# An attention and expert kernel: a new order of loads, slots and units in its first third

## The chip, the cores and the metric

The kernel runs on one core of a Trainium2 chip. The metric is device time in microseconds (us) of one execution. TensorE multiplies matrices, VectorE (DVE in the rows), ScalarE (ACT) and GpSimd (POOL) work element by element, and SyncE (SP) issues the loads. Each of them executes its instructions in a fixed order, and an instruction that waits holds back all behind it on that engine. For SP this means that a load that waits for its buffer holds back all later loads.

## The reference

Three blocks follow each other. The input is q, k, v of shape (4 batches, 8 heads, 576 positions, 64).

```
q_d, k_d, v_d = means over groups of 4 positions        # 144 positions
out_up    = repeat(softmax(q_d k_d^T / 8) v_d, 4)
out_local = softmax(q k^T / 8 where |i - j| < 4) v
x = (out_up + out_local)  as 2304 tokens x 512
x = (sigmoid(x w_gate) * (x w_val)) w_out                # 512 -> 1536 -> 512
logits = x phi                                           # 32 slots, 8 experts x 4
d = softmax of logits over the tokens;  slot_in = d^T x
slot_out[e] = relu(slot_in[e] w1[e]) w2[e]
result = softmax of logits over the slots  times slot_out
```

The weights w_gate, w_val and w_out arrive as 64-bit floats; the kernel converts them itself.

## The kernel before

*Attention.* Two heads make a pair; there are 4 pairs (NP) in a batch, numbered k = 0 to 15. The downsampled attention of a pair is `g_items(k)`: load, pool the groups of four (`g_pool`: q and k by reductions on VectorE or additions on POOL, v on POOL), scores (psD), three exponentials on ScalarE, transposes (psE), product with v (psV), copy to od. The local attention of a tile t of 128 tokens is `l_items(t)` or `attend(t)`: load lq, lk, lv (`load_tile`), scores (psS), mask and softmax in the tile t, transposes (psT), product with lv (psO), sum with od into x, and the split of x into a high part xh (ScalarE) and a low part xl (POOL).

*Units.* The first expert layer is cut into 6 chunks u of 256 columns (w_gate and w_val together 512 columns). `unit(t, u)` is 12 matmuls of 512 columns into psM: high times high, high times low and low times high over four blocks of 128 rows; then a tanh on ScalarE and one step on VectorE give h. Before that, `load_w(u)` loads the chunk's raw 64-bit values and `prep_w` converts them, in four pieces of a chunk: one step on ScalarE and three on VectorE (`to_f32`, result wf), a cast to whi on ScalarE, and the rest wlo on POOL.

*wo.* The last weights are loaded in 12 blocks of 128 rows (`load_wo`, `prep_wp`), converted in the same way, written to a buffer in main memory (wod), transposed (psW), multiplied with phi, and closed after every fourth block.

*Slots.* The pool wp has 12 slots of 2048 floats per partition. Each of whi and wlo of a chunk takes one for good. The pairs of batches 0 and 1 take two each, for a time, so later chunks wait for slots that pairs give back. The raw weights have 4 buffers of 512 KB, wf has 3, lq and lk together 4, lv one, the tile t two.

*Order.* The program text runs: loads of pairs 0 to 3 and tile 0, the four pairs, tile 0; then for each chunk u the loads of the next chunk and the next tile, the preparation, one or two of the pairs 4 to 7, the next tile, and the units that have become possible. Chunks 4 and 5 are prepared but their units come later, between the blocks of wo, which are scheduled with a higher priority. After that tiles 4 to 14 go through all six chunks in a hand-made order of half-units, with the work of other tiles beside them, then the tail with w1 and w2. A scheduler may move instructions ahead on each engine where nothing forbids it, but the loads marked by `keep_in_program_order` keep their order on SP, and so do TensorE's instructions from tile 4's units on.

Of the kernel before, what the change touches and what calls it, by code (L numbers as in the profile page):

```python
# [15 lines left out]
P = 128  # L16
# [6 lines left out]
def kernel(  # L23
# [91 lines left out]
    HPAIRS = ()  # L115
    odb = {}
    QP = 2 * NP

    def load_pair(k):
        b, p = divmod(k, NP)  # L120
        d = G[k] = {}
        if b < 2:
            pl, tag = (hp, "h") if k in HPAIRS else (wp, "w")
            m = pl.tile([P, 1536], F32, name="g0", tag=tag)
            o = 2 * S
            d["q"], d["k"] = m[:, :S], m[:, S:o]
            d["td"] = m[:, :3 * SD].rearrange("p (b w) -> p b w", w=SD)
            d["qd"], d["kd"] = m[:, o:o + 160], m[:, o + 160:o + 160 + SD]
            m = pl.tile([P, 1536], F32, name="g1", tag=tag)[:KH]
            v = m[:, :8 * P].rearrange("g (c r e) -> g c r e", c=2, r=4)  # L130
            d["v"] = [v[:, c] for c in range(2)]
            d["pt"] = m[:, :6 * P].rearrange("g (c b q) -> g c b q", c=2, b=3)
            d["vd"] = m[:, 8 * P:10 * P].rearrange("g (c e) -> g c e", c=2)
        else:
            gl = st["gl"]
            d["q"] = gl.tile([P, S], F32, name="gq", tag="gq")
            d["k"] = gl.tile([P, S], F32, name="gk", tag="gk")
            v = gl.tile([KH, 2, 4, P], F32, name="gv", tag="gv")
            d["v"] = [v[:, c] for c in range(2)]
            d["pt"] = gl.tile([KH, 2, 3, P], F32, name="gpt", tag="gpt")  # L140
            d["qd"] = gl.tile([P, 160], F32, name="qd", tag="qd")
            d["kd"] = gl.tile([P, SD], F32, name="kd", tag="kd")
            d["vd"] = gl.tile([KH, 2, P], F32, name="vd", tag="vd")
            d["td"] = gl.tile([P, 3, SD], F32, name="td", tag="td")
# [19 lines left out]
    def g_pool(k):  # L164
# [4 lines left out]
        for c in range(2):  # L169
            v = d["v"][c]  # L170
            nc.gpsimd.tensor_tensor(out=v[:, 0:2], in0=v[:, 0:2], in1=v[:, 2:4], op=ALU.add)
            nc.gpsimd.tensor_tensor(out=d["vd"][:, c], in0=v[:, 0], in1=v[:, 1], op=ALU.add)
# [40 lines left out]
    def g_av(k):  # L213
# [3 lines left out]
        for c in range(2):  # L217
            for h in range(2):
                r = slice(64 * h, 64 * h + 64)
                tmm(  # L220
                    ps[r, :SD], lhsT=d["vd"][:, c, r], rhs=d["pt"][:, c, :, 64 * h:64 * h + 48],
# [865 lines left out]
```

## Time and profile before

| | |
|---|---|
| median of 3 runs | 642.84 us (642.78 to 646.41) |
| the profiled execution | 645.25 us |
| its span, first to last instruction | 643.4 us |
| TensorE busy | 565.2 us (88%) |
| VectorE, ScalarE, POOL busy | 259.3, 261.9, 122.7 us |
| DMA | 93.50 MB, mean 145 GB/s |
| chain of waits, by engine | PE 65%, DVE 11%, DMA 8%, ACT 8%, SPq 3%, issue 3% |

The page gives busy times over the whole span and the chain that ended last. The kernel has stages with different limits, so the windows (busy time of each engine in a stretch) and the timeline (instructions in order of time) are read beside the page. A count such as x102 is the number of instructions in a group; a releaser is what an instruction waited for last.

### The profile page before, as it was taken

The numbers are of one execution on the slowest core, as the hardware profiler recorded it, in microseconds if no ns is written. First come the engines' busy times: TensorE is split into PE (matmuls) and PEld (weight loads), VectorE is DVE, ScalarE is ACT, GpSimd is POOL, SyncE is SP. The second block draws the span as 40 slices with busy tenths as digits, with TensorE's granted clock in tenths as the row PEclk, the third lists the DMA queues.
The fourth block names the chain that finished last, engine by engine and source line by source line (L and its number), as shares of the span: only waits on it lengthen the run. The fifth ranks groups of instructions, "written<-read, shape, count | busy, mean of one in ns | idle before, by whom it ended". The sixth has DMA issues, their size and how long they took to land.

```text
span 643.4 us, 11691 instructions
## 1 busy us (share of the span) xinstructions
PE 565.2 (88%) x4595; PEld 420.5 (65%) x4595; DVE 259.3 (40%) x596; ACT 261.9 (41%) x856; POOL 122.7 (19%) x169
## 2 busy tenths in 40 slices
PE   2557686888958999999999999999999999998974
PEld 2445564666835677777777777877877777763343
DVE  3697739464357233334243243233233211133032
ACT  2376253644345335355354443444243321133132
POOL 3343526431000332113032121000000100000000
PEclk9957787899975699999999999999999999999997
DMA  8846744260379423113032121182000276659999
GB/s 224 227 135 201 219 122 139 73 200 0 86 256 331 150 69 90 52 56 108 1 107 64 48 70 36 20 262 53 19 1 19 93 284 236 238 213 357 366 299 286
DMA packets 86230, 93.50 MB, mean 145 GB/s; under 512 B 8392, under 2 KB 65864, under 8 KB 86176
## 3 DMA queue, kind: packets, MB, share of 16 engines
q1 hardware_dynamic: 79904, 88.43, 44.4%
q10 hardware_dynamic: 6272, 4.33, 2.1%
q8 instruction: 36, 0.59, 0.4%
q14 instruction: 18, 0.15, 0.1%
HBM read 84.88 MB, written 7.86 MB: 144 GB/s over the span
## 4 chain that ended last, share of the span: by engine, by line
PE 65%; DVE 11%; DMA 8%; ACT 8%; SPq 3%; issue 3%; POOL 0%; ACTq 0%; DVEq 0%; POOLq 0%
PE psM L99 39%; PE psL L99 5%; PE psO L99 4%; ACT t L313 4%; PE psH L104 4%; SPq L109 3%; PE psT L104 2%; DVE wf L398 2%; PE psEH L99 2%; DMA g<-in_kT_dram 2%; DVE wf L401 2%; DVE wf L397 2%; PE psS L99 2%; DMA raw<-in_wg_dram 2%; PE psW L99 1%
## 5 line engine op out<-in xcount | busy, mean ns | idle before, releaser
L99 PE MATMUL psM<-whi,xh 128*128 128x512 f32 x432 | 185.5, 429 | 16.3 <-DVE h L484 8.3
L99 PE MATMUL psM<-whi,xl 128*128 128x512 f32 x432 | 173.6, 403 | 4.7 <-POOL xl L374 4.7
L99 PE MATMUL psM<-wlo,xh 128*128 128x512 f32 x432 | 174.2, 403 | 0.0
L99 PEld LDWEIGHTS psM<-whi,xh 128*128 128x128 f32 x432 | 83.4, 193 | 44.7 <-DVE h L484 11.4
L484 DVE SCALAR_TENSOR_TENSOR h<-th,psM 128x256 f32<-128x256 f32 x108 | 44.8, 416 | 157.5 <-ACT th L483 155.3
L99 PEld LDWEIGHTS psM<-whi,xl 128*128 128x128 f32 x432 | 83.1, 192 | 26.6 <-POOL xl L374 6.3
L483 ACT ACTIVATE th<-psM 128x256 f32<-128x256 f32 x108 | 40.9, 382 | 139.7 <-PE psM L99 139.2
L99 PEld LDWEIGHTS psM<-wlo,xh 128*128 128x128 f32 x432 | 83.6, 194 | 15.0 <-issue 0.6
L313 ACT ACTIVATE t<-t,mxl 128x70 f32<-128x70 f32 x144 | 48.9, 341 | 26.7 <-DVE mxl L302 26.4
L374 POOL TENSOR_TENSOR xl<-x,xh 128x512 fp32r<-128x512 f32 x18 | 23.8, 1324 | 160.6 <-ACT xh L373 160.6
L501 ACT COPY hT<-psH 128x512 f32<-128x512 f32 x54 | 31.7, 586 | 31.2 <-PE psH L104 30.8
L432 POOL TENSOR_TENSOR wlo<-wf,whi 128x512 fp32r<-128x512 f32 x24 | 33.6, 1407 | 36.3 <-ACT whi L431 35.3
L104 PE MATMUL psH<-ident,h 128*128 128x128 f32 x216 | 34.5, 281 | 1.0 <-ACT hT L501 0.8
L396 ACT ACTIVATE wf<-raw 128x512 f32<-128x512 f32 x36 | 24.1, 672 | 22.0 <-DMA raw<-in_wg_dram 12.6
L401 DVE SCALAR_TENSOR_TENSOR wf<-raw,wf 128x512 uint32<-128x512 uint32 x36 | 31.9, 889 | 0.8
L104 PEld LDWEIGHTS psH<-ident,h 128*128 128x128 f32 x216 | 25.9, 144 | 8.3 <-ACT hT L501 1.5
L398 DVE SCALAR_TENSOR_TENSOR wf<-raw,wf 128x512 uint32<-128x512 uint32 x36 | 28.5, 792 | 0.8
L397 DVE TENSOR_SCALAR wf<-wf 128x512 uint32<-128x512 uint32 x36 | 20.6, 574 | 18.1 <-ACT wf L396 17.9
L313 ACT ACTIVATION_READ_ACCUMULATOR t<-t,mxl 128x1 f32 x144 | 27.0, 187 | 0.0
L99 PEld LDWEIGHTS psS<-lk,lq 64*64 64x64 f32 x576 | 22.2, 143 | 5.9 <-issue 5.4
L99 PE MATMUL psS<-lk,lq 64*64 64x70 f32 x576 | 25.4, 236 | 0.0
L335 ACT COPY pt<-psT 70x512 f32<-70x512 f32 x36 | 19.4, 583 | 11.9 <-PE psT L104 11.6
(137 smaller groups left out, 718.3 us busy)
## 6 DMA issues: line engine op xcount, KB each, us to landing
ew<-in_w_dram SPq DMA_DIRECT2D x15, 1024.0 KB
raw<-in_wg_dram SPq DMA_DIRECT2D x12, 512.0 KB
raw<-in_wv_dram SPq DMA_DIRECT2D x12, 512.0 KB
raw<-in_wo_dram SPq DMA_DIRECT2D x12, 512.0 KB
ewp<-in_w_dram SPq DMA_DIRECT2D x22, 256.0 KB
lv<-in_vp_dram SPq DMA_DIRECT2D x16, 280.0 KB
lk<-in_kT_dram SPq DMA_DIRECT2D x16, 268.0 KB
lq<-in_qT_dram SPq DMA_DIRECT2D x16, 256.0 KB
```

The source lines that it names most:

```text
L99: ins = nc.tensor.matmul(*args, **kw)
L104: ins = nc.tensor.transpose(*args)
L313: nc.scalar.activation(out=tt[:, i], in_=tt[:, i], func=AF.Exp, bias=d["mx"][:, i:i + 1], accum_out=d["sl"][:, i:i + 1])
L374: nc.gpsimd.tensor_tensor(out=xl[t], in0=x, in1=xh[t].bitcast(F32), op=ALU.subtract)
L396: nc.scalar.activation(out=dst, in_=hi.bitcast(F32), func=AF.Copy, scale=2.0 ** -112)
L397: nc.vector.tensor_scalar(out=u, in0=u, scalar1=3, scalar2=None, op0=ALU.logical_shift_left)
L398: nc.vector.scalar_tensor_tensor(out=u, in0=lo, scalar=29, in1=u, op0=ALU.logical_shift_right, op1=ALU.bitwise_or)
L401: nc.vector.scalar_tensor_tensor(out=u, in0=hi, scalar=0x80000000, in1=u, op0=ALU.bitwise_and, op1=ALU.bitwise_or)
L432: nc.gpsimd.tensor_tensor(out=wlo[u][:, :, sl], in0=f, in1=whi[u][:, :, sl].bitcast(F32), op=ALU.subtract)
L483: nc.scalar.activation(out=th, in_=ps[:, :FU], func=AF.Tanh, scale=0.5)
L484: nc.vector.scalar_tensor_tensor(out=hs[t][:, u * FU:(u + 1) * FU], in0=th, scalar=1.0, in1=ps[:, FU:], op0=ALU.add, op1=ALU.mult)
L501: nc.scalar.copy(out=d[i], in_=ps.rearrange("p (j q) -> p j q", q=P))
```

## The change

The first third is written anew; the main part and the tail keep their text.

- Pairs 0 to 7 take one slot each (`load_qk`), and the values of all four pairs of a batch are loaded at once into two slots (`load_v`) and pooled by four wide additions on POOL (`v_pool`).
- A raw weight load takes 256 columns at once: rows of 2 KB, two buffers of 1 MB. `load_wo` takes two blocks at once.
- lv has two buffers, the tile t one.
- The loop over chunks is written out: after each preparation the next chunk's load and a tile's load are issued, pairs 4 to 7 are loaded together ahead of chunk 3 and worked together behind tile 3, units run by chunk, the units of chunk 4 run before wo, those of chunk 5 beside it. The blocks of wo have no priority of their own and their first loads stand ahead of tile 5's.

```
+    def load_qk(k):
+        b, p = divmod(k, NP)
+        d = G[k] = {}
+        m = wp.tile([P, 2048], F32, name="g0", tag="w")
...
+        load(d["q"], qT[b, p])
+        load(d["k"], kT[b, p, :, 3:3 + S])
+    def load_v(b):
+        for c in range(2):
+            v = GV[b, c] = wp.tile([P, 4 * DM], F32, name="g1", tag="w")[:KH].rearrange("g (r e) -> g r e", r=4)
+            load(v, vp[b, 3 + c * 4 * KH:3 + (c + 1) * 4 * KH, :].rearrange("(g r) e -> g r e", r=4))
+    def v_pool(b):
+        for c in range(2):
+            v = GV[b, c]
+            nc.gpsimd.tensor_tensor(out=v[:, 0:2], in0=v[:, 0:2], in1=v[:, 2:4], op=ALU.add)
+            nc.gpsimd.tensor_tensor(out=v[:, 2], in0=v[:, 0], in1=v[:, 1], op=ALU.add)
...
-        d["v"] = ld.tile([KW, 2, DM], F32, name="lv", tag="lv", bufs=1)
+        d["v"] = ld.tile([KW, 2, DM], F32, name="lv", tag="lv", bufs=2)
...
-            d["t"] = sf.tile([P, 2, NP, KW], F32, name="t", tag="t", bufs=2)
+            d["t"] = sf.tile([P, 2, NP, KW], F32, name="t", tag="t")
...
-            for h in range(2):
-                raw = raws[u, g, h] = stg.tile([P, NC, HU, 2], U32, name="raw", tag="raw", bufs=4)
+            raw = raws[u, g] = stg.tile([P, NC, FU, 2], U32, name="raw", tag="raw", bufs=2)
...
-        raw = raws[f] = stg.tile([P, DM, 2], U32, name="raw", tag="raw", bufs=4)
+        raw = raws[f] = stg.tile([P, 2, DM, 2], U32, name="raw", tag="raw", bufs=2)
...
+    attend(0); prep_chunk(0); load_w(1); load_tile(2); unit(0, 0)
+    attend(1); prep_chunk(1); load_w(2); load_tile(3)
+    for t, u in ((0, 1), (1, 0), (1, 1)):
+        unit(t, u)
+    for k in range(NP, 2 * NP):
+        load_qk(k)
+        if k == NP + 1:
+            load_v(1)
+    attend(2); prep_chunk(2); load_w(3)
+    for t, u in ((0, 2), (1, 2), (2, 0), (2, 1), (2, 2)):
+        unit(t, u)
+    v_pool(1)
+    attend(3)
+    for k in range(NP, 2 * NP):
+        for it in g_items(k):
+            it()
+        unit(K0 - 1, k - NP) if k < NP + 3 else None
+    prep_chunk(3); load_w(4)
...
+    for t in range(K0):
+        unit(t, 3)
+    prep_chunk(4); load_w(5)
+    for t in range(K0):
+        unit(t, 4)
+    prep_chunk(5)
+    load_wo(0); load_wo(2)
     for t in range(K0, TS):
         for it in list(l_items(t))[:-1]:
             it()
...
     for t in range(K0):
-        for u in range(UL, NU):
-            unit(t, u)
...
+        unit(t, NU - 1)
+        for f in range(3 * t, 3 * t + 3):
+            prep_wp(f)
+            if f % 2 and f + 3 < NF:
+                load_wo(f + 3)
```

(Calls that stand on lines of their own are joined by semicolons in the last part.)

The order of instructions, at three places. First SP's queue where the last chunk and wo are loaded; raw are the weights, lq, lk, lv a tile's inputs. Before:

```order
L109 DMA raw<-in_wg_dram 128x4x256 x2
L109 DMA raw<-in_wv_dram 128x4x256 x2
L109 DMA lq<-in_qT_dram 128x4x128
L109 DMA lk<-in_kT_dram 128x4x134
L109 DMA lv<-in_vp_dram 70x2x512
L109 DMA lq<-in_qT_dram 128x4x128
L109 DMA lk<-in_kT_dram 128x4x134
L109 DMA lq<-in_qT_dram 128x4x128
L109 DMA lk<-in_kT_dram 128x4x134
L109 DMA lv<-in_vp_dram 70x2x512
L109 DMA raw<-in_wo_dram 128x1024 x4
```

and now:

```order
L109 DMA raw<-in_wg_dram 128x4x512
L109 DMA raw<-in_wv_dram 128x4x512
L109 DMA sel_95<-in_cst_dram 128x128
L109 DMA phis<-in_phi_dram 128x4x32
L109 DMA raw<-in_wg_dram 128x4x512
L109 DMA raw<-in_wv_dram 128x4x512
L109 DMA raw<-in_wo_dram 128x2x1024 x2
L109 DMA lq<-in_qT_dram 128x4x128
L109 DMA lk<-in_kT_dram 128x4x134
L109 DMA lv<-in_vp_dram 70x2x512
```

The two loads of chunk 5 had three tiles with their lq, lk and lv, or parts of them, between them and wo; now wo follows chunk 5 at once, and nothing of a tile stands between chunks 4 and 5 either.

Second VectorE where pairs 4 to 7 are pooled (g_... are the pairs; L158 is now L173, the last step of a conversion L401 is now L416). Before, around pair 4:

```order
L401 SCALAR_TENSOR_TENSOR wf<-raw,wf 128x512 x2
L359 TENSOR_TENSOR x<-psO,od 128x512
L158 TENSOR_REDUCE g_487<-g_487 128x144
L397 TENSOR_SCALAR wf<-wf 128x512
L398 SCALAR_TENSOR_TENSOR wf<-raw,wf 128x512
L401 SCALAR_TENSOR_TENSOR wf<-raw,wf 128x512
```

and now, around pairs 6 and 7:

```order
L412 TENSOR_SCALAR wf<-wf 128x512
L498 SCALAR_TENSOR_TENSOR h<-th,psM 128x256
L413 SCALAR_TENSOR_TENSOR wf<-raw,wf 128x512
L173 TENSOR_REDUCE g_589<-g_589 128x144
L416 SCALAR_TENSOR_TENSOR wf<-raw,wf 128x512
L304 SCALAR_TENSOR_TENSOR t<-psS,mask 128x280
L374 TENSOR_TENSOR x<-psO,od 128x512
L173 TENSOR_REDUCE g_592<-g_592 128x144
L304 SCALAR_TENSOR_TENSOR t<-psS,mask 128x280
```

The conversion's last step stood ahead of the only pooling there; now the pooling of pair 6 stands between the last two steps of a conversion, and that of pair 7 between the two mask steps (L304) of a tile.

Third TensorE in the stage of wo: psW are the blocks of wo, whi and wlo a chunk's weights in the units. Before:

```order
L99 MATMUL psM<-wlo_397,xh 128x512
L99 MATMUL psM<-whi_396,xl 128x512
L104 MATMUL psW<-ident,wf 128x128 x4
L99 MATMUL psW_1475<-hT,phis 32x128 x4
L104 MATMUL psW<-ident,wf 128x128 x8
L99 MATMUL psW_1475<-hT,phis 32x128 x4
L104 MATMUL psW<-ident,wf 128x128 x4
L99 MATMUL psW_1475<-hT,phis 32x128 x4
```

and now, from the sixth of the twelve blocks:

```order
L99 MATMUL psO<-pt,lv 64x64 x16
L99 MATMUL psW_1471<-sel_95,part 128x32 x4
L99 MATMUL psW_1571<-hT,phis 32x128 x4
L104 MATMUL psW<-ident,wf 128x128 x3
L99 MATMUL psM<-whi_1261,xh 128x512
L99 MATMUL psM<-wlo_1262,xh 128x512
L99 MATMUL psM<-whi_1261,xl 128x512
L104 MATMUL psW<-ident,wf 128x128 x4
L99 MATMUL psW_1571<-hT,phis 32x128 x4
```

Before, the blocks stood together without a unit between them; now six units stand between the first six blocks, here the last three matmuls of them, and the later blocks follow alone.

## Rows read from the trace of the kernel before

**Rows 1.** Windows: stretch, busy us (instructions) per engine, clock, DMA share, GB/s.

```profile
0.00:221.00 221.00, 161.75 (x1151) 121.17 (x1152) 130.69 (x234) 101.80 (x307) 71.26 (x88) 0.81 0.57 169
221.00:643.40 422.40, 403.46 (x3447) 299.34 (x3446) 128.57 (x362) 160.12 (x549) 51.40 (x82) 0.99 0.42 133
147.00:181.00 34.00, 32.46 (x255) 25.87 (x254) 11.60 (x27) 12.38 (x48) 3.45 (x3) 1.00 0.17 41
181.00:214.00 33.00, 22.65 (x154) 14.81 (x154) 22.90 (x41) 18.61 (x45) 1.30 (x1) 0.57 0.86 303
```

**Rows 2.** Timeline: start us, length us, engine, line, instruction [idle before <-releaser].

```profile
25.97 0.69 ACT L396 ACTIVATE wf<-raw 128x512 f32<-128x512 f32 x1
...
205.05 1.12 PE L104 MATMUL psW<-ident,wf 128*128 128x128 f32 x4
...
206.90 0.66 PE L99 MATMUL psW<-hT,phis 128*32 128x128 f32 x8 [0.73 <-ACT hT L445]
...
220.95 0.64 PE L104 MATMUL psH<-ident,h 128*128 128x128 f32 x4
```

**Rows 3.** Waits of SP's queue, head: total us, times, longest us.

```profile
SPq L109 <- PE psO L99: 81.8, 6, 25.2
```

**Rows 4.** Timeline of SP's queue, consecutive issues around two loads of lv.

```profile
135.32 2.45 SPq L109 DMA_DIRECT2D lk<-in_kT_dram  x1
163.06 0.36 SPq L109 DMA_DIRECT2D lv<-in_vp_dram  x1
...
179.87 0.36 SPq L109 DMA_DIRECT2D lv<-in_vp_dram  x1
```

**Rows 5.** Instructions by form, head: count, busy us, mean ns, idle before.

```profile
L432 POOL TENSOR_TENSOR wlo<-wf,whi 128x512 fp32r<-128x512 f32 x24 | 33.6, 1407 | 36.3 <-ACT whi L431 35.3 <-PE psV L99 1.0
L401 DVE SCALAR_TENSOR_TENSOR wf<-raw,wf 128x512 uint32<-128x512 uint32 x36 | 31.9, 889 | 0.8
L398 DVE SCALAR_TENSOR_TENSOR wf<-raw,wf 128x512 uint32<-128x512 uint32 x36 | 28.5, 792 | 0.8
...
L397 DVE TENSOR_SCALAR wf<-wf 128x512 uint32<-128x512 uint32 x36 | 20.6, 574 | 18.1 <-ACT wf L396 17.9
...
L171 POOL TENSOR_TENSOR g<-g 72x256 f32<-72x256 f32 x16 | 12.9, 813 | 16.9 <-DMA g<-in_vp_dram 16.8
...
L191 ACT ACTIVATE g<-psD,mxd 128x144 f32<-128x144 f32 x24 | 8.9, 377 | 28.7 <-DVE mxd L188 26.3 <-PE psS L99 1.2 <-issue 1.2
...
L211 ACT COPY g<-psE 72x384 f32<-72x384 f32 x16 | 7.0, 475 | 4.8 <-PE psE L104 4.6 <-issue 0.2
...
L191 ACT ACTIVATION_READ_ACCUMULATOR g<-psD,mxd 128x1 f32 x24 | 4.8, 199 | 0.0
```

**Rows 6.** Timeline: a load's issue and its first reader.

```profile
115.42 0.34 SPq L109 DMA_DIRECT2D g<-in_qT_dram  x1
...
118.15 0.75 DVE L158 TENSOR_REDUCE g<-g 128x144 f32<-128x576 f32 x1 [0.80 <-DMA g<-in_qT_dram]
```

**Rows 7.** Windows of loading: weight rows, wo rows, wo with stores.

```profile
52.00:57.00 5.00, 5.00 (x13) 3.56 (x14) 2.06 (x6) 4.06 (x19) 1.72 (x2) 0.58 1.07 343
182.00:186.00 4.00, 0.54 (x3) 0.10 (x1) 0.62 (x2) 3.53 (x17) 0.60 (x1) 0.99 1.02 369
190.00:206.00 16.00, 12.86 (x92) 8.38 (x92) 11.40 (x20) 7.76 (x14) 0.00 (x0) 0.50 0.92 325
```

**Rows 8.** Chain of waits: start us, length us, piece, instructions.

```profile
161.94 1.08 PE psO L99 x32
...
174.54 4.21 PE psM L99 x18
...
217.85 2.46 PE psM L99 x6
```

**Rows 9.** Timeline: three casts of a chunk's weights.

```profile
89.55 1.66 ACT L431 CAST whi<-wf 128x512 fp32r<-128x512 f32 x3
```

More of the change, by code (lines that the diff above doesn't have):

```diff
@@ L168, in g_pool @@
         pool4(nc.vector if k < NP else nc.gpsimd, d["kd"], d["k"])
[L169 removed]
+        for c in range(2) if k >= QP else ():
             v = d["v"][c]
             nc.gpsimd.tensor_tensor(out=v[:, 0:2], in0=v[:, 0:2], in1=v[:, 2:4], op=ALU.add)
[L172 removed]
+            nc.gpsimd.tensor_tensor(out=d["vd"][c], in0=v[:, 0], in1=v[:, 1], op=ALU.add)
     def g_scores(k):
@@ L663, with prep_chunk @@
     nc.scalar.activation(out=warm, in_=warm, func=AF.Exp)
-    load_pair(0)
-    load_pair(1)
-    load(mask.rearrange("p b w -> p (b w)"), cst[:, 2 * P:2 * P + 3 * KW])
-    load_tile(0)
-    load_pair(2)
-    load_pair(3)
-    load_w(0)
-    load(sel4, cst[:, P:2 * P])
-    load(phis, phi.rearrange("(c p) s -> p c s", p=P))
-    for k in range(NP):
-        for it in g_items(k):
-            it()
-    attend(0)
-    early = {1: [4], 2: [5, 6], 3: [7]}
-    UL = NU - 2
-    for u in range(NU):
-        if u + 1 < NU:
-            load_w(u + 1)
-        if u + 1 < K0:
-            load_tile(u + 1)
+    def prep_chunk(u):
         for g in range(2):
@@ L687 @@
                 prep_w(u, g, h)
-        for k in early.get(u, []):
-            load_pair(k)
-        if u >= UL:
-            continue
-        if 0 < u < K0:
-            attend(u)
-        for k in early.get(u, []):
-            for it in g_items(k):
-                it()
-        for t in range(min(u, K0)):
-            unit(t, u)
-        if u < K0:
-            for v in range(u + 1):
-                unit(u, v)
+    load_qk(0)
+    load_qk(1)
+    load_v(0)
+    load_qk(2)
+    load_qk(3)
+    load(mask.rearrange("p b w -> p (b w)"), cst[:, 2 * P:2 * P + 3 * KW])
+    load_tile(0)
+    load_w(0)
+    load_tile(1)
+    for k in range(NP):
+        items = list(g_items(k))
+        if k == 0:
+            items.insert(1, lambda: v_pool(0))
+        for it in items:
+            it()
+    attend(0)
+    prep_chunk(0)
+    load_w(1)
+    load_tile(2)
+    unit(0, 0)
+    attend(1)
+    prep_chunk(1)
+    load_w(2)
+    load_tile(3)
+    for t, u in ((0, 1), (1, 0), (1, 1)):
[4 more added lines that the diff above has]
+            load_v(1)
+    attend(2)
+    prep_chunk(2)
+    load_w(3)
+    for t, u in ((0, 2), (1, 2), (2, 0), (2, 1), (2, 2)):
[4 more added lines that the diff above has]
+        for it in g_items(k):
+            it()
+        unit(K0 - 1, k - NP) if k < NP + 3 else None
+    prep_chunk(3)
+    load_w(4)
+    load(sel4, cst[:, P:2 * P])
+    load(phis, phi.rearrange("(c p) s -> p c s", p=P))
+    for t in range(K0):
+        unit(t, 3)
+    prep_chunk(4)
+    load_w(5)
+    for t in range(K0):
+        unit(t, 4)
+    prep_chunk(5)
+    load_wo(0)
+    load_wo(2)
     for t in range(K0, TS):
```

73 lines of the change are left out of this document (28 added, 45 removed).

## The prediction

> **What bounds the kernel now.** I read the windows first. Up to 221 us no engine is full: TensorE is busy for 161.75 us, VectorE for 130.69, ScalarE for 101.80, and the DMA engines for a share of 0.57. From 221 us to the end TensorE is busy for 403.46 of 422.40 us [rows 1]. So there is a head, which is a chain of waits, and a main part, which is TensorE's own work. The diff is in the head only. The order of TensorE's instructions is the same in both kernels from the psH transposes on that start at 220.95 us before [rows 2]; I call this start the boundary. The forecast is the boundary's new time plus an unchanged rest.
>
> Next I asked what the head waits for. The list of waits says that SP, which issues every load in program order, stood 81.8 us in six waits for a psO matmul of TensorE [rows 3]. SP's rows in order of time show the two longest: after 135.32 nothing until 163.06, and then 179.87 [rows 4]. Both end with a load of lv. There was one lv buffer, so tile t+1's values wait until tile t's psO has read them, and everything behind that load in the queue waits too, the weights of the next chunk and wo included. The cost is plain in the windows: in 147 to 181 us TensorE is busy for 32.46 of 34 us while DMA runs at a share of 0.17; in 181 to 214 the roles are exchanged, DMA 0.86, TensorE 22.65 of 33 at a clock of 0.57 [rows 1]. Units and the preparation of wo stand one after the other.
>
> **The change, part by part, as times in the head.**
>
> *Start.* Before, the first weight conversion starts at 25.97 us [rows 2]. Ahead of the first weights the queue now has the same four pairs with all values of the batch, and a first weight load of 1024 instead of 512 KB. I take 26 us for both. The additions on POOL become four of 1024 and 512 columns; nothing shows these, so by proportion to 256 columns at 0.81 us [rows 5] they take at most 3.2 + 3.2 + 1.6 + 1.6 = 9.6 us, and at least a half of it if a fixed part dominates. They end near 20 us, when TensorE has no weights for another 25 us: hidden; uncovered they would cost at most their own length.
>
> *Chunk period.* A preparation costs VectorE 0.57 + 0.79 + 0.89 = 2.26 us (with POOL's interference in it), POOL 1.41 [rows 5]. Two preparations empty one raw buffer: 4.5 us. Its refill costs a fixed part and the bytes. The fixed part: a 288 KB load issued at 115.42 is used at 118.15 [rows 6]; 2.7 us less 1.0 for its bytes leaves 1.75. The rate: 1 KB rows of weights ran at 343 GB/s at a DMA share of 1.07, 4 KB rows of wo at 369 at 1.02 [rows 7], which is 320 and 360 at a share of one. For the new 2 KB rows I take 350, near the upper: 1.05 MB in 3.0 us, refill 4.75, period 4.5 + 4.75 = 9.3 us per chunk. (The Trainium skill, DMA: Bandwidth & Descriptors, Specifications, has transfers at line rate from 512 bytes on, so wider rows would gain nothing. At 320 the five refills on the path would cost 0.3 us more each, 1.5 us in all. The two rows here differ by more than that rule allows, though by little.)
>
> *Chunks 0 to 2.* Chunk 0 from 26 to 35 us. The refill issued at 30.5 shares the engines with tile 1 and lands at 37; chunk 1, with 3 us of tile 0's attention on VectorE, ends at 47. The second lv buffer lets chunk 2's load go when tile 0's psO is done, about 43; chunk 2 begins at 49 and, with tile 1's attention, would end at 61. Here the new order costs time. lv of tile 3 waits for tile 1's psO, about 59, and pairs 4 to 7 are behind it. On VectorE the last step of chunk 2's fourth preparation now stands behind the pooling of pair 6, whose q lands after lv and two pairs and all values: 2.9 MB at 300 GB/s and 1.75, so 70.5. Before, a single pair's pooling stood there. Chunk 2 ends at 72, and on POOL behind the two wide additions at 77.
>
> *Pairs 4 to 7 and chunk 3.* From 77, units (0,2), (1,2), (2,0) to (2,2) at 2.8 us each and tile 3's 2 us: 93. A matmul of a unit takes 4.21 / 18 = 0.23 us at full clock and 2.46 / 6 = 0.41 near half [rows 8]; 12 make the 2.8. Then four pairs and tile 4 go through ScalarE: per pair three exponentials at 0.38 with 0.20 for their sums, two copies at 0.48 [rows 5] and one shorter copy, 3.0 us; tile 4's eight exponentials 4.6, and three of the units' tanh 1.1; 17.7 us, to 111, with units (3,0) to (3,2) beside them. Chunk 3's weights need slots of these pairs: its casts wait for them, as before, where three waited for pair 4 until 89.55 [rows 9]. With the fourth preparation 2.3, cast 0.6 and POOL 1.4, chunk 3 is ready at 115.
>
> *Chunks 4 and 5.* The second half of chunk 4 is loaded when that preparation frees its buffer, 113; it lands at 118 and is prepared at 122. Chunk 5 follows by a period: 131, on POOL 133. No lv stands between.
>
> *wo.* Its loads are now ahead of tile 5's in SP's order and take the buffers that chunk 5 leaves: the first is issued near 127 and lands at 132. Per pair of rows' blocks: 1.05 MB read and 0.52 written at 325 GB/s [rows 7] plus 1.75 is 6.6 us, and preparing two is 3.6 without POOL plus a unit's 0.4 twice, 4.4; two buffers make 5.5 us per pair, six pairs end at 165. The bytes agree: 6.3 + 3.1 + 2.4 (tiles 5 to 7) = 11.8 MB from 127 us, 36 us, 163. TensorE agrees: from 131 it has six units (17 us), tile 5 (three groups like psO's 1.08 [rows 8], 3.3) and twelve blocks of psW, each 1.12 + 0.66 at half clock [rows 2] and near 1.0 at full, with three closing steps 15: 166. I take 165. Behind the last preparation stand psW, two copies, four small matmuls and a closing step, about 5 us from the same rows: 170. Then two halves of unit (4,0), psS, psH and half of (4,1), which before ran ahead of it: 6.5 us. The boundary is at 177.
>
> *The rest.* sel4 and phis come later, but still ahead of chunk 5's load, and are first used in wo's blocks. One t buffer instead of two makes tile t+1's mask step wait for tile t's psT; in the main part the psT is placed six half-units ahead of it, so nothing; uncovered, about a psT, 1 us, for each of 12 tiles. The half-sized pairs and batch values only move slots.
>
> **Sum.** 220.95 - 177 = 44 us. The profiled execution took 645.25 us, 2.4 above the median of 642.84. 645.25 - 44 = 601; from the median, 599. I say 600.
>
> **Rivals.**
> - *Better overlap.* Tile 1's psO comes at 55 instead of 59, chunk 2 and all behind it are 4 us earlier, pairs' bytes go at 350 (2 us), and wo's 11.8 MB at 355 (3 us) with 3 less at the chunk turns. Boundary 165, time 588. For it: the bytes of the whole head, 169 GB/s over 221 us [rows 1] or 37 MB, need only 125 us at 300. Against: nearly every step waits for a step on another engine.
> - *The clock takes half back.* From chunk 3 on TensorE waits for preparations and for wo. In 190 to 206 us before, it was busy for 12.86 of 16 us and had 0.50 of its clock, that is 1.2 GHz [rows 7]; in 147 to 181, almost without waits, 1.00 [rows 1]. If half of the 12 units and of the blocks run at 1.2 GHz, that is 13 us for units (72 x 0.18) and 7 for the blocks and tile 5: boundary 197, time 621.
> - *The clock takes all of it, slower.* The same at 1.2 GHz throughout from 115: units 59, tile 5 6, blocks 12 x (1.12 + 0.66) and three closing steps of 1, 25; with 12 of waits and 12 to the boundary: 229, time 653. It decides from a mean granted clock under about 0.53 in that stretch. The Trainium skill (TensorE: Matmul & The Clock Gate, Part 1) says that the throttled state is the default and that activity releases it, and the row of 190 to 206 fits that; by that rule waits alone could hold the whole stretch at 1.2 GHz. Against: six units in a row at full clock without a wait (147 to 181) are in this order too, (0,3) to (1,4).
> - *Nothing gained.* Half-way between these two, the later slots cost what the earlier wo brings: boundary 215 to 222, 639 to 646.
>
> **Chances.** Forecast 0.58 (its own range 590 to 612), better overlap 0.16, half taken back 0.16 (612 to 632), nothing 0.05, slower 0.05. The range 584 to 622 leaves out the last two, half of the third, and a little of the second, some 0.2. A measurement of this kernel tells about 1% from no change. Faster by over 1%: 0.90, within: 0.05, slower: 0.05.
>
> **What would show it.** SP: no wait over 10 us for psO after 60 us; the first load of wo issued near 127. VectorE: the last step of chunk 2 held by a q load until about 70 us. ScalarE: chunk 3's first three casts between 95 and 105. Weights of chunk 5 ready at 133, last preparation of wo at 165, boundary at 177, main part 422 us as before. The forecast is wrong if the clock in 114 to 170 is near 0.5, if chunk 3 is ready later than 125, or if the main part does not keep its 422 us.

## The result, and the profile after

The changed kernel takes 635.72 us (median of 4 executions, 632.55 to 636.76) beside 643.56 us for the kernel before on the same chip: a ratio of 0.9862, with a 95% interval of 0.9815 to 0.9909. It is faster by 1.4%, and the whole interval lies below 1. The forecast was 600 us with a range of 584 to 622, so the direction was right and the size was not, and the time lies outside the range: 8 us were gained where 44 were expected.

The profiled execution took 636.76 us, its span is 634.9. The page of the profile gives the busy time of each engine and, in part 4, the shares of the chain that ended last:

```profile
PE 570.7 (90%) x4595; PEld 422.4 (67%) x4595; DVE 258.5 (41%) x596; ACT 260.2 (41%) x856; POOL 118.3 (19%) x145
...
PE 62%; DMA 14%; DVE 11%; ACT 9%; issue 2%; SPq 1%; POOL 0%; ACTq 0%; DVEq 0%
```

The boundary, the psH transposes from which TensorE's order is the same in both kernels, is the second row here (timeline of TensorE; the bracket is the idle time before it and who ended it):

```profile
206.33 0.60 PE L104 MATMUL psH<-ident,h 128*128 128x128 f32 x4
209.43 0.66 PE L104 MATMUL psH<-ident,h 128*128 128x128 f32 x4 [1.10 <-ACT hT L515]
```

It moved from 220.95 [rows 2] to 209.43 us, by 11.5, where the forecast had 177. The main part behind it takes 425.5 us and took 422.4 [rows 1]. So the loss is in the head, with 3 us in the main part. The windows (length, busy time of each engine with its instructions, granted clock, DMA share, GB/s), two of them cut at 47 us, when the forecast has chunk 1 ready:

```profile
0.00:209.40 209.40, 163.75 (x1150) 120.57 (x1150) 128.12 (x233) 100.84 (x308) 71.90 (x72) 0.89 0.61 184
209.40:634.90 425.50, 406.99 (x3445) 301.88 (x3445) 130.34 (x364) 159.39 (x548) 46.38 (x73) 0.98 0.41 129
...
47.00:209.40 162.40, 136.27 (x942) 102.39 (x942) 96.20 (x177) 78.11 (x237) 53.78 (x53) 0.85 0.55 173
```

and the same cut of the kernel before:

```profile
47.00:221.00 174.00, 140.05 (x982) 105.16 (x982) 100.02 (x180) 79.78 (x237) 52.34 (x57) 0.81 0.52 160
```

TensorE is the thing to see: from 47 us on it is busy for 136 of 162 us. The forecast ended the head at 177, which leaves 130.

**Where SP waits now.** List of SP's waits in the first 210 us (in total, times, longest):

```profile
SPq L109 <- DVE wf L416: 85.4, 10, 37.5
SPq L109 <- PE psO L99: 14.9, 2, 8.7
```

The waits on psO fell from 81.8 [rows 3] to 14.9. In their place SP waits 85.4 for VectorE to finish a weight preparation, 37.5 of it at once. In the kernel before these waits were short:

```profile
SPq L109 <- DVE wf L401: 20.1, 6, 5.6
```

SP's rows in order of time show where (weights only):

```profile
90.64 0.37 SPq L109 DMA_DIRECT2D raw<-in_wg_dram  x1
128.59 0.37 SPq L109 DMA_DIRECT2D raw<-in_wv_dram  x1
131.50 0.37 SPq L109 DMA_DIRECT2D raw<-in_wg_dram  x1
139.00 0.36 SPq L109 DMA_DIRECT2D raw<-in_wv_dram  x1
145.23 7.23 SPq L109 DMA_DIRECT2D raw<-in_wo_dram  x2
```

The second half of chunk 4 is held from 90.64 to 128.59. Its buffer is free when chunk 3's fourth preparation has read it. That one has no wf buffer, since the three wf hold preparations that wait to be cast (whi, on ScalarE) and to give their rest (wlo, on POOL). Both need slots of the pairs, and the pairs' scores stand behind units on TensorE. The chain on TensorE, ScalarE, POOL and ScalarE again, where the last row is the first step of the fourth preparation:

```profile
103.14 2.42 PE L99 MATMUL psD<-g 64*64 64x144 f32 x36
...
117.42 1.66 ACT L445 CAST whi<-wf 128x512 fp32r<-128x512 f32 x3
...
120.96 3.71 POOL L446 TENSOR_TENSOR wlo<-wf,whi 128x512 fp32r<-128x512 f32 x3 [14.88 <-PE psV L99]
...
124.24 1.22 ACT L411 ACTIVATE wf<-raw 128x512 f32<-128x512 f32 x2
```

In the kernel before, the like of the second row, the casts of chunk 3, stood at 89.55 [rows 9]: chunk 3's casts come 28 us later than they did.

### The profile page after: what moved, and what is told of

The parts are those of the page before. It is cut to its first block, busy times and chain, and to the rows that moved or that the text cites. A ratio compares the mean times of both kernels' runs of the same rounds, so it can differ in the third digit from the quotient of the medians.

```text
span 634.9 us, 11572 instructions
## 1 busy us (share of the span) xinstructions
PE 570.7 (90%) x4595; PEld 422.4 (67%) x4595; DVE 258.5 (41%) x596; ACT 260.2 (41%) x856; POOL 118.3 (19%) x145
## 4 chain that ended last, share of the span: by engine, by line
PE 62%; DMA 14%; DVE 11%; ACT 9%; issue 2%; SPq 1%; POOL 0%; ACTq 0%; DVEq 0%
PE psM L99 38%; PE psL L99 5%; ACT t L328 4%; PE psO L99 4%; PE psH L104 4%; DMA raw<-in_wv_dram 4%; DMA g<-in_qT_dram 3%; PE psEH L99 2%; DMA raw<-in_wo_dram 2%; DMA g<-in_kT_dram 2%; PE psS L99 2%; DVE wf L416 2%; DVE wf L413 2%; PE psT L104 2%; DMA out_dram<-ob 2%
## 5 line engine op out<-in xcount | busy, mean ns | idle before, releaser
L446 POOL TENSOR_TENSOR wlo<-wf,whi 128x512 fp32r<-128x512 f32 x24 | 35.2, 1479 | 47.5 <-ACT whi L445 30.4
L416 DVE SCALAR_TENSOR_TENSOR wf<-raw,wf 128x512 uint32<-128x512 uint32 x36 | 30.6, 855 | 0.4
L413 DVE SCALAR_TENSOR_TENSOR wf<-raw,wf 128x512 uint32<-128x512 uint32 x36 | 28.4, 791 | 0.4
L99 PE MATMUL psS<-lk,lq 64*64 64x70 f32 x576 | 27.0, 247 | 0.0
L99 PE MATMUL psO<-pt,lv 70*64 70x64 f32 x576 | 23.8, 240 | 3.0 <-ACT pt L350 3.0
```

What stands on the lines that cost most here:

```text
L99: ins = nc.tensor.matmul(*args, **kw)
L413: nc.vector.scalar_tensor_tensor(out=u, in0=lo, scalar=29, in1=u, op0=ALU.logical_shift_right, op1=ALU.bitwise_or)
L416: nc.vector.scalar_tensor_tensor(out=u, in0=hi, scalar=0x80000000, in1=u, op0=ALU.bitwise_and, op1=ALU.bitwise_or)
L446: nc.gpsimd.tensor_tensor(out=wlo[u][:, :, sl], in0=f, in1=whi[u][:, :, sl].bitcast(F32), op=ALU.subtract)
```

## The experiments

All kernels in one table. Ratios are to the kernel before, measured beside each of them (its medians lie between 643.56 and 648.24), with 95% intervals; the last three columns are times in the profiled execution (us): the first load of wo is issued, the last weight conversion starts on VectorE, the boundary.

| kernel | median us | ratio | first wo | last conv. | boundary |
|---|---|---|---|---|---|
| before | 643.56 | 1 | 180.3 | 212.9 | 220.95 |
| changed | 635.72 | 0.986 (0.982–0.991) | 145.2 | 192.3 | 209.43 |
| q4 | 626.40 | 0.970 (0.964–0.975) | 138.5 | 189.5 | 200.20 |
| wf4 | 621.09 | 0.962 (0.956–0.967) | 140.3 | 181.6 | 195.43 |
| pf | 630.37 | 0.977 (0.972–0.982) | 124.3 | 192.2 | 203.40 |
| lv1 | 636.12 | 0.984 (0.977–0.991) | 149.4 | 193.8 | 210.72 |
| wfp | 630.68 | 0.975 (0.971–0.980) | 122.7 | 188.6 | 201.70 |
| qwf | 622.79 | 0.963 (0.959–0.967) | 137.9 | 182.8 | 196.12 |
| blv | 620.54 | 0.959 (0.953–0.965) | 146.3 | 185.5 | 196.47 |
| bwf4 | 652.68 | 1.011 (1.006–1.016) | 181.8 | 216.6 | 225.31 |
| bh | 627.56 | 0.969 (0.963–0.975) | 145.9 | 189.5 | 199.95 |
| bhw | 624.40 | 0.964 (0.958–0.970) | 145.3 | 187.3 | 197.87 |
| awo | 628.84 | 0.970 (0.963–0.978) | 144.6 | 193.1 | 200.16 |
| blvwf | 620.60 | 0.959 (0.952–0.966) | 143.7 | 182.0 | 192.25 |
| blvl | 607.07 | 0.938 (0.930–0.946) | 135.3 | 174.4 | 183.08 |
| afl | 619.93 | 0.959 (0.952–0.966) | 135.3 | 177.0 | 191.80 |
| awowf | 616.85 | 0.955 (0.949–0.962) | 139.8 | 182.9 | 191.26 |
| qawowf | 621.78 | 0.963 (0.956–0.970) | 137.7 | 178.5 | 194.14 |

### What holds chunk 4: quarters, a fourth wf buffer, earlier pairs

**q4**, four raw buffers of 512 KB:

```diff
-            raw = raws[u, g] = stg.tile([P, NC, FU, 2], U32, name="raw", tag="raw", bufs=2)
...
+            for h in range(2):
+                raw = raws[u, g, h] = stg.tile([P, NC, HU, 2], U32, name="raw", tag="raw", bufs=4)
+                c0 = (u * FU + h * HU) * 2
...
-        raw = raws[f] = stg.tile([P, 2, DM, 2], U32, name="raw", tag="raw", bufs=2)
...
+        raw = raws[f] = stg.tile([P, DM, 2], U32, name="raw", tag="raw", bufs=4)
...
```

> The changed kernel with its weights loaded as before: four raw buffers of 512 KB (rows of 1 KB, one wo block each) in place of two of 1 MB; the order of all loads and everything else stay. Theory COARSE (the 1 MB buffers hold loads back: the second half of chunk 4 stood behind one unprepared quarter of chunk 3 from 90.6 to 128.6, and each wo buffer waits for two blocks): three of chunk 4's four quarters are issued by about 95, only the fourth near 128; the DVE's wait of 3.0 before chunk 4's second half goes; the wo stage, 145.2 to 193.0 = 47.8, falls to about 38, the start of the common part from 209.4 to 193 to 198, the kernel to 620 to 626. Theory SLOTS (the late end of the four pairs of batch 1 holds chunk 3's casts, and all else follows from them): chunk 3's casts stay at 117, the common part starts at 204 to 208, 630 to 635. Theory WIDE ROWS HELP (narrow rows cost what the change meant to save): wo stage and weight loads longer, 638 to 645.

Measured 626.40. SP's row of the held load, with the wait inside a group of two:

```profile
88.92 37.71 SPq L109 DMA_DIRECT2D raw<-in_wv_dram  x2
```

Three quarters of chunk 4 now go by 89 and only the fourth stays behind, until 126, as COARSE said. That brings the first wo load 6.8 forward. The size is nearer to COARSE's than to SLOTS's (0.4 us above the range of the one, 3.6 below the other's), the place is not: the boundary, 200.20, lies between the two ranges, and from the first wo load to the last conversion it is 51.0, no less than the changed kernel's 47.1; the boundary comes earlier because less is left behind the last conversion (10.7 instead of 17.1).

**wf4**, one more wf buffer (two places alike):

```diff
-        f = stg.tile([P, NC, HU], F32, name="wf", tag="wf")
+        f = stg.tile([P, NC, HU], F32, name="wf", tag="wf", bufs=4)
```

> The changed kernel with four wf buffers in place of three. Theory SLOTS: the fourth preparation of chunk 3 no longer needs a cast to end first, so it ends near 93, the second half of chunk 4 is loaded then and not at 128.6, but the casts of chunk 3 still wait for the pairs' slots until 117; chunk 4 is prepared 3 to 5 sooner. In the wo stage ScalarE's wait of 4.2 for a store of wod goes, for a further 4 or so. Common part from 209.4 to 199 to 203: 626 to 630. Theory COARSE: the load that was held comes free in the same way, so as much as the quarters bring ahead of 145, but the wo buffers of two blocks stay: 628 to 632. Theory CLOCK (TensorE at the lower level, not the preparations, sets 70 to 210): no change, 634 to 637.

Measured 621.09, more gained than any theory expected, and mostly in the way that SLOTS describes. SP's rows:

```profile
89.94 0.37 SPq L109 DMA_DIRECT2D raw<-in_wg_dram  x1
94.94 0.37 SPq L109 DMA_DIRECT2D raw<-in_wv_dram  x1
128.54 0.37 SPq L109 DMA_DIRECT2D raw<-in_wg_dram  x1
132.76 0.37 SPq L109 DMA_DIRECT2D raw<-in_wv_dram  x1
140.34 4.86 SPq L109 DMA_DIRECT2D raw<-in_wo_dram  x2
```

The held load goes at 94.94 and not at 128.59, but the first wo load only 4.9 earlier than in the changed kernel. The wo stage, from there to the last conversion, falls from 47.1 to 41.2, and what follows it to the boundary from 17.1 to 13.9. In the changed kernel a conversion of that stage had waited for a store to wod, which held one of the three wf (timeline of ScalarE):

```profile
163.79 0.67 ACT L411 ACTIVATE wf<-raw 128x512 f32<-128x512 f32 x1 [4.17 <-DMA wod<-wf]
```

**pf**, the pairs of batch 1 ahead of chunk 2's units and of tile 3:

```diff
-    for t, u in ((0, 2), (1, 2), (2, 0), (2, 1), (2, 2)):
-        unit(t, u)
     v_pool(1)
-    attend(3)
     for k in range(NP, 2 * NP):
         for it in g_items(k):
             it()
-        unit(K0 - 1, k - NP) if k < NP + 3 else None
+    for t, u in ((0, 2), (1, 2), (2, 0), (2, 1), (2, 2)):
+        unit(t, u)
+    attend(3)
+    for u in range(3):
+        unit(K0 - 1, u)
```

> The changed kernel with the four pairs of batch 1 written ahead of chunk 2's units and ahead of tile 3 (in the change they stand behind both). Theory SLOTS: their scores start near 78 in place of 103, chunk 3's first casts come near 92 in place of 117.4, the second half of chunk 4 is loaded near 97 in place of 128.6; tile 3 and its three units go behind them and cost TensorE some 8 that were hidden; chunk 5 is prepared 12 to 18 sooner, and with the wo stage as it is the common part starts at 192 to 198: 618 to 625. Theory COARSE: the wait moves with the casts, but the wo stage keeps its 48: 622 to 628. Theory CLOCK: TensorE has the same matmuls, at a lower level if its queue is thinner: 632 to 640.

Measured 630.37: short of both theories on the preparations. The preparations came further forward than the 12 to 18 expected, the first wo load is at 124.3, 21 earlier. And yet the boundary is only 6 earlier. A window, two rows of TensorE and two of ScalarE tell why:

```profile
140.00:180.00 40.00, 40.00 (x277) 29.74 (x275) 15.56 (x34) 14.07 (x41) 2.59 (x2) 1.00 0.51 164
```

```profile
139.08 0.60 PE L104 MATMUL psW<-ident,wf 128*128 128x128 f32 x4
...
161.14 1.09 PE L104 MATMUL psW<-ident,wf 128*128 128x128 f32 x8
```

```profile
144.27 0.68 ACT L411 ACTIVATE wf<-raw 128x512 f32<-128x512 f32 x1 [3.97 <-DMA wod<-wf]
...
162.48 0.67 ACT L411 ACTIVATE wf<-raw 128x512 f32<-128x512 f32 x1
```

From 140 to 180 TensorE is busy all the time at a granted clock of 1.00, 2.4 GHz, while VectorE and ScalarE are idle for more than half of it. A wo block gives its wf back only when TensorE has transposed it, and in TensorE's order those transposes stand behind units: the first block is transposed at 139.08, the next two at 161.14, and between 144.27 and 162.48 no conversion begins. None of the three theories had that; CLOCK had TensorE as the limit, but at the lower level.

**wfp** (both) and **qwf** (quarters and four wf):

> The changed kernel with four wf buffers and the pairs of batch 1 ahead of chunk 2's units and tile 3, the two edits that gave 14.6 and 5.3 alone (635.7 to 621.1 and to 630.4). Theory SAME CAUSE (both free the fourth preparation of chunk 3; the rest of what four buffers give is in the wo stage): with the pairs early the casts are early, so the two gains overlap in chunk 3 and add only what the fourth buffer does in the wo stage, which alone took 65 in the run with the pairs first: common part at 188 to 194, 613 to 620. Theory TENSORE (with the preparations early, TensorE has no idle time left between 130 and 200 and sets the start): no better than four buffers alone, 619 to 626. Theory INDEPENDENT (gains add): 613 to 617.

> The changed kernel with four raw buffers of 512 KB and four wf buffers (alone: 626.4 and 621.1 of 635.7). Theory WF (what the quarters gave, they gave by letting three loads pass the fourth preparation; with a fourth wf buffer there is nothing left to pass): the same as four wf buffers alone within 3, 618 to 624. Theory COARSE (each raw buffer of two wo blocks holds the next load by itself): wo stage shorter by another 5 to 8, 612 to 617. Theory WIDE ROWS HELP: 624 to 630.

wfp at 630.68 is worse than wf4 alone and past the range of every theory. Its first wo load is the earliest of all, 122.7, and its boundary 201.70. The moved pairs cost something ahead of that: between 100 and 120 TensorE is busy for only 9.95 of 20 us at a clock of 0.71 (19.47 at 1.00 in the changed kernel), and its longest wait there, 9.59, is for the softmax of tile 3, which now stands behind the pairs (4.60 in pf):

```profile
116.36 1.89 PE L104 MATMUL psT<-ident,t 128*70 128x128 f32 x8 [9.59 <-DVE t L338]
```

How much of the loss this wait makes was not tried. qwf is wf4 within the intervals: with a fourth wf there is nothing left for quarters to pass, as WF said.

### The parts of the change alone

**lv1** undoes the second lv buffer in the changed kernel, **blv** makes it alone in the kernel before:

```diff
-        d["v"] = ld.tile([KW, 2, DM], F32, name="lv", tag="lv", bufs=1)
+        d["v"] = ld.tile([KW, 2, DM], F32, name="lv", tag="lv", bufs=2)
...
-            d["t"] = sf.tile([P, 2, NP, KW], F32, name="t", tag="t", bufs=2)
+            d["t"] = sf.tile([P, 2, NP, KW], F32, name="t", tag="t")
```

> The changed kernel with the v tile's second buffer and the single t buffer undone (one lv, two t, as before). Theory of the prediction (the second lv buffer takes away SP's waits on psO, 81.8 in three waits before): the weight loads stand behind the v tile again, SP's waits on psO return with 15 to 35 more, and chunks 1 to 3 come 5 to 12 later each: 641 to 650, about the time before the change. Rival (the order of the loads has put each v tile behind the psO that it waits for anyway; the next chunk's buffer is the later wait): 634 to 638.

> The kernel before with the change's second lv buffer (and one t buffer for it) alone. By the prediction SP's three waits on psO, 81.8 in all (25.2 the longest), set the preparations before the change; with a second buffer most of that goes and the wo stage starts 15 to 30 sooner: 615 to 630. Rival, after the run in which the same buffer was taken out of the changed kernel at no cost (636.1 against 635.7): the waits on psO go and SP waits at the next place, the raw buffers and the pairs' slots: within 1% of before, 638 to 646.

The same two lines are worth nothing in one kernel and 4.1% in the other. (The 81.8 us of waits that both expectations name are six waits, as in the prediction, and not three. The t buffer was not tried without the lv buffer; the waits below are the lv buffer's.) SP's waits in the first 210 us of lv1:

```profile
SPq L109 <- DVE wf L416: 62.5, 8, 28.8
SPq L109 <- PE psO L99: 47.1, 4, 20.0
```

and of blv:

```profile
SPq L109 <- DVE wf L401: 47.4, 12, 14.3
SPq L109 <- PE psO L99: 30.5, 3, 20.5
```

In lv1 the psO waits come back with 32 more, as the prediction's theory had it, but the waits for wf fall by 23: most of what waits for psO would have waited for wf anyway. In blv 51 of the 81.8 go; the waits for wf grow by 27 from 20.1, in pieces of up to 14.3. The first wo load moves from 180.3 to 146.3. So the prediction's main cause was right for the kernel before, and this part alone brings 26 us; the rest of the change costs some 17 of them again.

**bh** adds the head to blv (a batch's values at once, a pair in one slot; pairs and all else in the old order), **bhw** the 1 MB buffers too:

> The kernel before with the second lv buffer and the change's head: a batch's values loaded at once, a pair in one slot in place of two; order of the program, quarters of 512 KB and wo stage as before. With the lv buffer alone the ratio to before was 0.959 (620.5), with all of the change 0.986. Theory ORDER (what is lost again lies in the new order: the four pairs together and late, units by chunk, wo preparations behind units): the head costs nothing and frees eight slots, so chunk 3 needs no pair slots: ratio 0.945 to 0.962, 611 to 622. Theory HEAD (waiting for all four pairs' values, and two slots held until the last pair, is what costs): 0.970 to 0.985. Theory TENSORE (from 80 to 180 TensorE is full with the lv buffer alone): 0.955 to 0.962, no change.

> The same with the change's raw buffers too: two of 1 MB in place of four of 512 KB, wo blocks in pairs. Only the order of the program is still that of before. Theory ORDER: within 1% of the run with the head alone. Theory COARSE (the 1 MB buffers cost by themselves, as in the changed kernel, where four quarters gave 9): 0.012 to 0.020 above it.

0.959, 0.969, 0.964 and, with the new order, 0.986. The head seems to cost about 0.010, which is not settled: the interval of bh, 0.963 to 0.975, overlaps that of blv by 0.002, and 0.969 lies between the ranges of ORDER and HEAD. The wide buffers cost nothing here: COARSE fails in the old order. The step that loses is the last one, the order: 0.022, with intervals that lie apart. On the rows of 2 KB the Trainium skill (DMA: Bandwidth & Descriptors, Specifications) has line rate from 512 bytes on, so no gain from width; the difference of 0.005 between bhw and bh lies inside both intervals and does not speak against it.

**awo** writes the end of the head as before:

```diff
-    for t in range(K0):
-        unit(t, 4)
     prep_chunk(5)
...
+    f = 0
     for t in range(K0):
-        unit(t, NU - 1)
-        for f in range(3 * t, 3 * t + 3):
-            prep_wp(f)
-            if f % 2 and f + 3 < NF:
-                load_wo(f + 3)
+        for u in (4, 5):
+            unit(t, u)
+            for _ in range(2):
+                if f < NF:
+                    prior(lambda: prep_wp(f))
...
```

> The changed kernel with the units of chunks 4 and 5 and the wo preparations written as before: chunk 5 prepared ahead of chunk 4's units, two preparations behind each unit and with priority. All else as changed. Theory ORDER, its wo part: the wo stage, 47.8 from first load to last preparation, falls to 35 to 40, the kernel to a ratio of 0.965 to 0.975 (622 to 629). Rival (the late pairs and chunk 3 make all of it; the wo stage is only shifted): 0.983 to 0.990, no change.

The ratio, 0.970, is the one that ORDER gave, by another way than it said: the wo stage does not shrink (144.6 to 193.1, 48.5 us). But the boundary follows the last conversion after 7.1 us instead of 17.1, since the units are done by then. So of the 0.022 that the order loses, the end of the head makes some 0.016. The rest, 0.006 between awo and bhw, lies within the intervals.

**bwf4** and **blvwf**, four wf in the kernel before and in blv:

> The kernel before with four wf buffers in place of three and nothing else. Theory THE CHANGE MADE IT (before the change the weights' loads stood behind psO, so wf was not what held them; the change's late pairs made wf the limit): within 1%, 638 to 646. Theory WF EVERYWHERE (three wf buffers hold the wo stage and the chunks in any order): 10 to 15 less, 628 to 634.

> The kernel before with the second lv buffer and four wf buffers. Alone the first gave a ratio of 0.959, the second 1.011 (slower). Theory WF EVERYWHERE (a fourth wf buffer helps wherever the loads are not held by psO): 0.945 to 0.953. Theory TENSORE (TensorE is full from 80 to 180 with the lv buffer, so earlier preparations give nothing): 0.955 to 0.963. Rival (four preparations ahead of casts put conversions before attention's steps on ScalarE and VectorE, as where it cost 1.1%): 0.965 to 0.975.

In blv the ratio stays, as TENSORE had it, though in the profiled execution the last conversion is 3.5 and the boundary 4.2 earlier. In the kernel before it costs 1.1%; neither theory had that. SP's waits on psO are as long as before (83.3 in 225 us), which the buffer does not touch; why it harms was not tried.

### Is TensorE the floor?

In **blvl** and **afl**, blv and the changed kernel leave out a third of the matmuls of the first four tiles' units, the term with the residue xl:

```diff
-            for a, w in ((xh, whi), (xh, wlo), (xl, whi)):
+            for a, w in ((xh, whi), (xh, wlo), (xl, whi))[:2 if t < K0 else 3]:
```

> The kernel before with the second lv buffer (ratio 0.959, common part at 196.5 in its profile), and a third of the units' matmuls of the first four tiles left out (the term of the residue of x; part of the computation): 24 units by 4 matmuls by 0.234 = 22.5 of TensorE's time at the full level, 15 of it after 80, where its profile shows TensorE full. Theory TENSORE (with the loads free of psO, TensorE's own work sets the start of the common part): start at 178 to 186, 604 to 612. Theory PREPARATIONS (conversions, stores and buffers still set it): 192 to 197, 617 to 622.

> The changed kernel with the same third of the units' matmuls of the first four tiles left out. Its profile has TensorE idle 2.8 at 182 to 185, 10.6 for DVE at 193 to 204 and the wo preparations as the later side. Theory PREPARATIONS: the work left out was beside them, start of the common part at 203 to 209, 629 to 636; less work may even lower the granted clock and give part of that back. Theory TENSORE: 190 to 198, 616 to 624.

The boundary falls by 13.4 in blv (196.47 to 183.08) and by 17.6 in the changed kernel (209.43 to 191.80). In both kernels the numbers of TENSORE come out. In blv TensorE is near full from 80 to 180, in the changed kernel less so (windows of blv, then of the changed kernel):

```profile
80.00:180.00 100.00, 94.36 (x723) 71.19 (x722) 65.14 (x125) 55.89 (x167) 31.51 (x33) 0.97 0.58 177
```

```profile
80.00:180.00 100.00, 89.21 (x592) 67.97 (x592) 64.60 (x119) 49.59 (x149) 27.00 (x22) 0.90 0.47 145
```

But in the changed kernel it is not only that TensorE is full: afl's SP rows show the preparations themselves coming earlier,

```profile
87.17 0.37 SPq L109 DMA_DIRECT2D raw<-in_wg_dram  x1
119.77 0.37 SPq L109 DMA_DIRECT2D raw<-in_wv_dram  x1
123.61 0.37 SPq L109 DMA_DIRECT2D raw<-in_wg_dram  x1
130.00 0.36 SPq L109 DMA_DIRECT2D raw<-in_wv_dram  x1
135.32 6.28 SPq L109 DMA_DIRECT2D raw<-in_wo_dram  x2
```

the held load by 8.8, the first wo load by 9.9, the last conversion by 15.3. In blvl they move too, the first wo load by 10.9 and the last conversion by 11.1. TensorE's units are links of the preparations' chain, ahead of the pairs and among the transposes of wo. A split in "TensorE" and "preparations" as two rivals was the wrong question.

**awowf** and **qawowf**, awo with four wf, and with quarters too:

> The changed kernel with the wo stage written as before and four wf buffers (alone 0.970 and 0.962 of before; the changed kernel 0.986). Theory TENSORE FLOOR (every version so far ends at 0.959 or above, since TensorE is full from about 100 on): 0.955 to 0.962. Theory ADD (the wf buffers free chunk 3, the order frees the wo stage): 0.944 to 0.952.

> The same with four raw buffers of 512 KB too, so that of the change's parts only the head, the second lv buffer, the order of the loads and the units by chunk up to chunk 3 are left. Theory TENSORE FLOOR: as the run without the quarters within 0.005. Theory COARSE: another 0.008 to 0.015 less.

awowf has the lowest median of the complete kernels, 616.85, faster than both kernels of this case; the intervals of awowf and blv (620.54) overlap. ADD's range is missed, though the interval reaches into it: the ratio, 0.955, is the lower end of TENSORE FLOOR's range. qawowf is 0.008 above it, where neither theory had it. In qawowf the last conversion is 4.4 earlier than in awowf and the boundary 2.9 later. The same cut of windows from 47 us to the boundary, of blv,

```profile
47.00:196.50 149.50, 129.84 (x965) 98.68 (x963) 98.82 (x178) 78.48 (x237) 53.01 (x58) 0.87 0.61 180
```

of afl,

```profile
47.00:191.80 144.80, 112.59 (x847) 82.59 (x847) 97.82 (x177) 78.16 (x237) 52.06 (x51) 0.80 0.60 188
```

of blvl,

```profile
47.00:183.10 136.10, 107.99 (x885) 82.90 (x885) 99.79 (x180) 77.04 (x237) 51.46 (x58) 0.84 0.66 200
```

and of awowf:

```profile
47.00:191.30 144.30, 126.73 (x943) 96.00 (x943) 94.08 (x173) 76.22 (x235) 48.31 (x45) 0.90 0.59 186
```

Busy time by granted clock is a rough estimate of TensorE's work at the full level: before 140.05 x 0.81 = 113, changed 116, blv 113, awowf 114, and 90 and 91 in afl and blvl, where 22.5 were taken out. By this estimate it is one amount of work, 113 to 116 us, and each kernel adds its own loss to it:

| from 47 us to the boundary | total | work | lower clock | idle |
|---|---|---|---|---|
| before | 174 | 113 | 27 | 34 |
| changed | 162 | 116 | 20 | 26 |
| blv | 150 | 113 | 17 | 20 |
| awowf | 144 | 114 | 13 | 18 |
| the forecast | 130 | 113 | 17 for both | |

(Lower clock is busy time less work, idle is total less busy time.) So over this whole stretch no kernel here has reached TensorE's work as a floor: awowf still loses 31 of its 144 us. A forecast that keeps the matmuls cannot go below it.

## Why the prediction was right and wrong

**Right.** The boundary's arithmetic: in all runs the rest behind it is 422 to 426 us, and what the boundary gains, the kernel gains. SP's waits on psO as a cost of the kernel before: blv, 4.1%. (One reading of them was wrong: the wait that ends at 179.87 is 13.1 long and the third; the second longest, 16.7, ends at 88.30, also with a load of lv.) No psO wait over 10 us (8.7), the first conversions at their old place, the last step of chunk 2 behind pair 6's load (forecast to end at 72, seen from 76.07 to 77.20). The direction was right, and that the whole change lies in the head.

**Where it went wrong,** by its own steps.

- *Chunks 0 to 2* came 3 to 4 late: chunk 1 was done on VectorE at 50.3 (forecast 47), chunk 2 on POOL at 81.3 (77). A small miss of many small terms.
- *Pairs 4 to 7 and chunk 3.* The step had five units and tile 3 take 16 us, 77 to 93, at the price of the full clock. They took 81.3 to 103.1, 22 us: the units' matmuls of 81 to 86 run at 0.43 us each, the lower level, behind a wait of 2.20 for this chunk, and those of 93 to 96 again, behind a wait of 1.94. Then ScalarE's stretch took 20.5 (105.0 to 125.5) and not 17.7. Casts were to come at 95 to 105 in what would show it, and came at 117.42. The walk did have this chain (pairs, slots, casts, fourth preparation, the 1 MB buffer, chunk 4's load); its links were sized as if nothing else stood in their queues. Chunk 3 was ready at about 130.9 (115). Lag by the load of chunk 4's second half: 15.6, from 113 to 128.59.
- *Chunk 5* and the first wo load: 127 forecast, 145.23 seen, 18 late, 2.6 of it new; 9.9 of the 18 go with a third of the units' matmuls (afl). Chunk 5 was ready at 154.2 (133).
- *wo.* Forecast 38 from the first load to the last conversion's end, seen 47.8. The term counted bytes, VectorE and TensorE each for itself and found that they agree at 163 to 166. It did not count that three wf buffers tie them together: a block's buffer is free only when its store has landed and TensorE has transposed it. A fourth wf took 6 off (wf4). What makes the other 4 is open.
- *Behind the last conversion* 12 were forecast (165 to 177), 16.4 seen from its end: TensorE still had the last two blocks' products, a closing step, two halves of unit (4,0), psS of tile 6 and half of (4,1) to do, as the step said, and ran at the lower level until 205.
- *The main part* was to stay at 422 and took 425.5 in the profile. Over all runs, with the same instructions, it is 422.0 to 426.3, so the 3 us cannot be put down to the change.

These terms add up to the 32 us between 177 and 209.43: 15.6, 2.6, 9.8 and 4.4. They say where the time went, not what it costs. pf has its first wo load at 124.3, earlier than the forecast's 127, and its boundary still is at 203.40, 79 us later and not 50.

**The step that failed: the sum that was left out.** Each step was walked on the engine that prepares; TensorE was summed for the wo stage alone, at the price of the full clock, and its total over the head was never held against the result. It was there to be read: 140 us of busy time from 47 us on at a clock of 0.81, in the estimate above some 113 at the full level. A boundary at 177 leaves 17 us in all for idle time and lower clock, and the walk itself left TensorE only three units, beside the small matmuls of the pairs and of tile 4, from 93 to 115. The changed kernel loses 46, and even the best complete kernel here 31.

**The rivals.** "The clock takes half back" (boundary 197, 621 us) has part of the mechanism: some 20 us of the changed kernel's head are lost to the lower level, but so are 27 before. From 114 to 170, where the prediction looked for it, the clock was 0.91; it was at 0.50 from 185 to 205, behind the last loads of wo. "Nothing gained" (boundary 215 to 222, 639 to 646) is nearest in cause, by its sentence that the later slots cost what the earlier wo brings; it was given 0.05. In time the result lies between the two, 3.7 above the 612 to 632 of the one and 3.3 below the other. Of the prediction's own signs that the forecast is wrong, the one on chunk 3 (ready later than 125) came true. "Slower" and "better overlap" are out.

## What to carry to other kernels

Before a walk through waits is believed, sum the work of the engine that everything passes through, at its full rate, and see how much idle time the forecast leaves for it; a forecast that leaves far less than the kernel before had needs a reason for it. When a wait is removed, follow the buffer behind it to whoever frees it, store and transposes included: here one more small buffer gave the changed kernel more than the whole change had given. And try a change's parts alone, since two lines of this one, in the kernel before, were worth three times the whole.

## What the hardware showed

The granted clock fell where TensorE had just waited. In the changed kernel TensorE waited 2.75 us for a copy at 182.8 to 185.5, and the stretch behind it ran at the lower level, 1.2 GHz, though TensorE was busy for 16.67 of the 20 us from 185 to 205. The copy itself stood on ScalarE behind a conversion that had waited 2.69 for a load of wo. The row of TensorE, and windows:

```profile
185.53 0.65 PE L99 MATMUL psW<-hT,phis 128*32 128x128 f32 x8 [2.75 <-ACT hT L459]
...
180.00:190.00 10.00, 6.81 (x60) 4.94 (x53) 4.26 (x9) 5.61 (x12) 1.30 (x1) 0.74 0.78 296
190.00:200.00 10.00, 7.64 (x53) 4.83 (x52) 2.93 (x5) 3.35 (x7) 1.41 (x4) 0.50 0.40 134
...
185.00:205.00 20.00, 16.67 (x119) 11.73 (x120) 7.82 (x15) 6.72 (x14) 5.11 (x10) 0.50 0.46 150
```

The Trainium skill (TensorE: Matmul & The Clock Gate, Part 1) has the throttled state as the default that activity releases. The fall behind the wait fits that; what kept the level low for the 20 us behind it, these rows do not show. Less work went with a lower clock: with a third of the unit matmuls gone the mean granted clock from 47 us to the boundary was 0.80 in afl beside 0.85 in the changed kernel (0.84 beside 0.87 in blvl and blv), and 23.7 us less of busy time shortened that stretch by 17.6.
